# A block's closing waits, moved in front of the last stores

## The chip, the cores and the metric

The kernel runs on one core of a Trainium2 chip. Such a core has five engines that run side by side, each from an instruction stream of its own: TensorE (PE, matrix products), VectorE (DVE), ScalarE (ACT), GpSimd (POOL) and SyncE (SP). SP computes nothing here: it issues nearly all DMA transfers and waits on semaphores. A DMA transfer that is issued runs on its own; when it has landed, it raises the semaphore that its issuing instruction names.

The metric is device time in microseconds (us) of one execution, as the median of several runs.

## The reference

The kernel computes a transformer block in which attention and a gated feed-forward part read the same normalised input and are added to it. `x` is 2048 x 512 in bf16, with 32 heads of width 16 and a feed-forward width of 1792.

```python
xn = _layernorm(x)
q, k, v = split(xn @ wqkv)                      # 32 heads of 16
p = softmax((q @ k.T) / 4)                      # 2048 x 2048 per head
attn = (p @ v).reshape(S, D) @ wo
gate, up = xn @ W_gate, xn @ W_up               # 512 -> 1792
glu = (where(gate > 0, gate, 0) * up) @ W_down  # 1792 -> 512
out = x + attn + glu
```

## The kernel before, in words

The program is not written engine by engine. `Graph.op` collects operations with their engine, an assumed duration and their dependencies; `Graph.run` plays them through and so fixes one queue for each engine; `Graph.emit` turns the queues into instructions, with semaphores where an operation needs another engine's result. What a queue's order is, is therefore decided before the kernel runs, and each engine walks its queue in that order.

The queries are worked off in four blocks of 512 rows (`NB`), within a block four groups of eight heads (`NGG`), each in two halves, and in each of those 16 tiles of 128 keys (`NT`). For each tile PE makes scores (`score`), ACT or, for a part of the tiles, DVE and POOL make the exponentials, and PE multiplies those with the values (`pv_stream`). Between these, as filler, PE does the projections, the gated feed-forward products and the output rows of the block before.

The output is stored in 16 tiles of 128 rows. Twelve of them, those of the first three blocks, are stored from SP's queue in the course of the kernel (`out_rows`, the store at L1122). The last four belong to the last block and form the kernel's tail (`normalise_last`, L1190 and on): for each tile the last product is added to what was accumulated, on DVE for three tiles (L1246) and by an ACT copy for the fourth (L1242). The three DVE tiles are stored by SP (L1256), the fourth by ACT's own queue (L1253, because `OWN_STORE = (3,)`).

Each transfer on SP belongs to a *stream*, a name that stands for one semaphore. A transfer that has no named stream gets one of its own (the weights and the input tiles, 50 with the eight transposing transfers); those that recur share a few: `("q", v, h)` for the query pieces (8), `("wu", k)` and `("wg", k)` for the feed-forward weights (8), `("n1", n)`, `("n2", n)`, `("n3", n, j)` for the softmax sums (24), `("pk", j, n)` for the packed heads (8), `("xr", m)` for the residual rows (4), `("out", m)` for the twelve earlier stores (8), and `("out", m, k)`, with three parts, for the three stores of the tail. That makes 113 streams on SP, and the ACT store has a semaphore of its own, `d_st0`: 114 in all.

A kernel must not end before its transfers have landed. `emit` sees to that with the list `fin`: one wait for each of the 114 semaphores, at that semaphore's final value. `play("SP", ...)` gives these waits to SP after the last operation of its queue (L560 to L562):

```python
            if e == "SP":
                for s, v in fin:
                    eng.wait_ge(s, v)
```

The program's end, an exchange of semaphores among all engines, carries line L564 in the profile, since that is where the block of engine programs opens.

Of the kernel before, what the change touches and what calls it, by code (L numbers as in the profile page):

```python
# [133 lines left out]
class Graph:  # L134
# [296 lines left out]
    def emit(self, nc, es):  # L431
# [18 lines left out]
        def line(o):  # L450
            return o.stream if o.eng == "SP" else "PEhi" if o.eng == "PE" and o.half else o.eng
        for e in self.ENGS:
            n = {}
# [10 lines left out]
        streams = {}  # L464
        while left:
            moved = False
            for e in self.ENGS:
                q = self.queue[e]
                while pos[e] < len(q):
                    o = q[pos[e]]  # L470
# [4 lines left out]
                    if e == "PE" and o.wsrc and o.load is not None:  # L475
                        o.wwaits = []
                        for d in sorted(o.wsrc, key=lambda d: -d.seq):
                            c = line(d)
                            v = d.val if d.eng == "SP" else d.cseq
# [7 lines left out]
                    for d in sorted(o.deps, key=lambda d: -d.seq):  # L487
                        c = line(d)
                        v = d.val if d.eng == "SP" else d.cseq
# [22 lines left out]
        dsem = {s: es.enter_context(nc.semaphore("d_%d" % i)) for i, s in enumerate(streams)}  # L512
        for e in self.ENGS:
            v = {}
            for o in self.queue[e]:
# [5 lines left out]
                elif o.signal:  # L521
                    v[line(o)] = v.get(line(o), 0) + 1
                    o.sem = (sems[line(o)], v[line(o)])
        fin = [(dsem[s], 16 * n) for s, n in streams.items()]
        stores = [o for o in self.queue["ACT"] if o.name == "st"]
        for i, o in enumerate(stores):
            fin.append((es.enter_context(nc.semaphore("d_st%d" % i)), 16))
# [2 lines left out]
        def play(e, eng):  # L530
            def wait(ds):
                best = {}
                for d in ds:
                    s, v = d.sem
                    if id(s) not in best or best[id(s)][1] < v:
                        best[id(s)] = (s, v)
                for s, v in best.values():
                    eng.wait_ge(s, v)
            loaded = set()
            for i, o in enumerate(self.queue[e]):  # L540
                if e == "PE" and o.load and o not in loaded:
                    wait(o.wwaits)
                    o.load(eng)
                if e == "PE" and o.load is not None and o.waits:

                    for q in self.queue[e][i + 1:i + 1 + self.AHEAD_LOADS]:
                        if q.load is None or q.wwaits or q in loaded:
                            break
                        if q.half != o.half:
                            if q.load:  # L550
                                q.load(eng)
                                loaded.add(q)
                            break
                wait(o.waits)
                ins = o.fn(eng)
                if e == "SP" or o.name == "st":
                    ins.then_inc(o.sem[0], 16)
                elif o.signal or o.pair is not None:
                    ins.then_inc(o.sem[0], 1)
# [4 lines that stand above are left out]
        with nc.Block() as block:  # L564
            @block.sync
            def _(e):
                play("SP", e)

            @block.gpsimd
            def _(e):  # L570
                play("POOL", e)

            @block.vector
            def _(e):
                play("DVE", e)

            @block.scalar
            def _(e):
                play("ACT", e)

            @block.tensor
            def _(e):
                play("PE", e)
# [934 lines left out]
```

## Time and profile before

| | us |
|---|---|
| median of 3 runs without a profile | 693.67 |
| the runs' lowest and highest | 692.96, 693.94 |
| the profiled execution | 697.19 |
| span in it, from the first to the last instruction | 695.2 |
| PE busy | 680.9 (98% of the span) |
| ACT busy | 671.4 (97%) |
| DVE busy | 601.6 (87%) |
| POOL busy | 505.0 (73%) |

The clock granted to TensorE was 0.999 of full speed. The profiled execution's own time stands above its span by 2.0 us, and above the median of the runs by 3.5 us.

How to read it: a row of the timeline gives an instruction's start from the span's beginning and its length. Rows that begin with SPq or ACTq are instructions of that engine's sequencer: waits, branches and DMA issues, which are not counted as busy time. A wait appears in the profile as `EVENT_SEMAPHORE`. For a DMA issue the row has the time that issuing took; how long the transfer then needed until its semaphore was complete stands apart, as "DMA to landing", counted from the issue. A line such as L562 is the line of the kernel's source that made the instruction.

### The profile page before, as it was taken

To read this page: it belongs to the slowest core of one execution; us is meant where nothing else is said; L and a number is where in the kernel's file an instruction comes from. 1 tells how busy PE (TensorE), PEld (TensorE's weight loads), DVE (VectorE), ACT (ScalarE), POOL (GpSimd) and SP (SyncE) were. 2 spreads that over 40 slices of the span, in tenths; PEclk is the share of its full clock that TensorE was granted. 3 is DMA by queue.
4 is the path that set the end of the run, shared out by engine and by line. 5 is a ranking of instruction groups with operands and counts; after the bars stand their busy time and mean duration, and the time that the engine had idled before them with its cause. 6 is when DMAs were issued, how large, how long until landed. Compare 5 with 4: busy or idle time off the path is not lost.

```text
span 695.2 us, 46400 instructions
## 1 busy us (share of the span) xinstructions
PE 680.9 (98%) x22230; PEld 388.8 (56%) x20952; DVE 601.6 (87%) x1009; ACT 671.4 (97%) x733; POOL 505.0 (73%) x513
## 2 busy tenths in 40 slices
PE   8999999999999999999999999999999999999997
PEld 3546566566554566556654644556554455565754
DVE  8958899999999686899999778899998787898795
ACT  6999999999999999999999999999999999999993
POOL 3323678777789876788868877888878966787790
PEclk9999999999999999999999999999999999999999
DMA  7230111233201122110101111111100121121001
GB/s 213 57 57 21 38 45 32 50 103 92 65 15 31 43 58 48 27 47 21 39 12 28 46 50 54 31 40 34 36 16 19 39 73 46 50 50 33 21 16 41
DMA packets 55820, 31.87 MB, mean 46 GB/s; under 512 B 21196, under 2 KB 53644, under 8 KB 55628
## 3 DMA queue, kind: packets, MB, share of 16 engines
q1 hardware_dynamic: 55484, 28.79, 16.1%
q8 instruction: 169, 2.77, 1.7%
q14 instruction: 23, 0.19, 0.1%
q10 hardware_dynamic: 144, 0.13, 0.1%
HBM read 22.28 MB, written 2.35 MB: 35 GB/s over the span
## 4 chain that ended last, share of the span: by engine, by line
PE 73%; ACT 21%; DVE 4%; issue 1%; DMA 0%; DVEq 0%; POOL 0%
PE ps L129 72%; ACT ring L1465 21%; DVE qd L1418 2%; DVE stats L778 1%; DVE xn_sb L791 0%; DMA x_sb<-in_A_x_dram 0%; DVE mv L779 0%; DVE xnT L832 0%; DVE qd L1438 0%; PE ps L1202 0%; DVE qT L1014 0%; DVE xn_sb L1246 0%; DVE vare L771 0%; DVE up_sb L1078 0%; DVEq L564 0%
## 5 line engine op out<-in xcount | busy, mean ns | idle before, releaser
L1465 ACT ACTIVATE ring<-ps 128x1024 bf16<-128x1024 f32 x720 | 665.0, 1110 | 7.1 <-PE ps L129 6.1
L1434 POOL TENSOR_TENSOR qd<-qd,ints 128x512 int32<-128x512 int32 x450 | 454.3, 1041 | 145.4 <-DVE qd L1418 67.9
L129 PE MATMUL ps<-qT,kT 64*32 64x512 bf16 x8192 | 466.3, 375 | 1.7 <-issue 0.4
L1418 DVE TENSOR_SCALAR qd<-ps 128x512 int16<-128x512 f32 x608 | 396.0, 684 | 64.7 <-PE ps L129 59.7
L129 PE MATMUL ps<-qd,v_aug 64*32 64x512 bf16 x3648 | 296.2, 375 | 1.2 <-issue 0.8
L129 PE MATMUL ps<-ring,v_aug 64*32 64x512 bf16 x2880 | 252.6, 375 | 0.6 <-issue 0.3
L1398 PEld LDWEIGHTS <-kT 64*32 64x32 bf16 x7952 | 170.8, 92 | 122.9 <-issue 38.3
L1370 PEld LDWEIGHTS <-v_aug 64*32 64x32 bf16 x5488 | 135.1, 92 | 73.2 <-issue 12.9
L129 PE MATMUL ps<-xnT,wus 64*32 64x512 bf16 x1792 | 137.1, 375 | 0.0
L129 PE MATMUL ps<-xnT,wgs 64*32 64x512 bf16 x1792 | 135.8, 375 | 0.5 <-DVE up_sb L1078 0.2
L1438 DVE TENSOR_SCALAR qd<-qd 128x2048 int16<-128x2048 int16 x79 | 61.6, 792 | 1.7 <-PE ps L129 1.5
L862 PEld LDWEIGHTS <-wus 64*32 64x32 bf16 x1792 | 44.1, 92 | 23.2 <-issue 2.9
L862 PEld LDWEIGHTS <-wgs 64*32 64x32 bf16 x1792 | 44.0, 92 | 22.5 <-issue 2.9
L862 PEld LDWEIGHTS <-hT 64*32 64x32 bf16 x1792 | 43.4, 92 | 23.5 <-issue 4.0
L129 PE MATMUL ps<-Wd,hT 64*32 64x512 bf16 x768 | 55.7, 375 | 0.7 <-DVE qd L1418 0.6
L129 PE MATMUL ps<-Wk,hT 64*32 64x512 bf16 x512 | 41.9, 376 | 0.4 <-issue 0.4
L1078 DVE COPY up_sb<-ps 128x512 f32<-128x512 f32 x56 | 38.2, 682 | 3.6 <-PE ps L129 3.5
L1082 DVE SCALAR_TENSOR_TENSOR hT<-ps,up_sb 128x512 bf16<-128x512 f32 x56 | 38.2, 682 | 2.2 <-PE ps L129 1.9
L129 PE MATMUL ps<-Wv,hT 64*32 64x512 bf16 x512 | 40.1, 376 | 0.0
L129 PE MATMUL ps<-Wo_p,x_sb 64*32 64x512 bf16 x480 | 38.9, 375 | 0.0
L129 PE MATMUL ps<-xnT,Wq 64*32 64x512 bf16 x480 | 36.7, 375 | 0.0
L129 PE MATMUL ps<-xnT,Wk 64*32 64x512 bf16 x480 | 34.0, 375 | 0.1
(73 smaller groups left out, 262.8 us busy)
## 6 DMA issues: line engine op xcount, KB each, us to landing
wus<-in_B_W_up_dram SPq DMA_DIRECT2D x38, 128.0 KB, 2.7
wgs<-in_B_W_gate_dram SPq DMA_DIRECT2D x38, 128.0 KB, 2.6
rb<-rec_scr SPq DMA_DIRECT2D x124, 32.0 KB, 2.8
xr_sb<-in_A_x_dram SPq DMA_DIRECT2D x16, 128.0 KB, 2.3
qT<-qf SPq DMA_DIRECT2D x120, 16.0 KB, 2.6
out_dram<-xn_sb SPq DMA_DIRECT2D x15, 128.0 KB, 1.8
x_sb<-in_A_x_dram SPq DMA_DIRECT2D x8, 128.0 KB, 2.7
x_sb<-oT SPq DMA_DIRECT2D x60, 16.0 KB, 2.7
```

Of the source, the lines that this page charges most:

```text
L129: return e.add_instruction(mybir.InstMatmult(name=e.bass.get_next_instruction_name(), engine=mybir.EngineType.PE, ins=[e.lower_ap(x), e.lo ...
L778: G.op("DVE", 580, lambda e, m=m: e.bn_stats(stats[:, m, :], xs(m)), reads=[t_xm[m]], writes=[t_st], prio=pr, order=last_xn if m == 4 else ())
L862: e.ldweights(w()[rows, 32 * j:32 * j + 32], tile_position=(rows.start, 32 * j))
L1078: G.op("DVE", 603, lambda e: e.tensor_copy(up_sb[:, tup.slot, :], bank_of(tu)), reads=[tu], writes=[tup], prio=-590)
L1082: G.op("DVE", 603, lambda e: e.scalar_tensor_tensor(out=hT[:, th.slot, :], in0=bank_of(tg), scalar=0.0, in1=up_sb[:, tup.slot, :], op0=ALU ...
L1370: e.ldweights(vs(j), tile_position=(64 * half, 32 * j))
L1398: e.ldweights(ks(m), tile_position=(64 * half, 32 * m))
L1418: G.op("DVE", 601, lambda e, j=j, tx=tx: e.tensor_scalar(qd[:, tq.slot, 512 * j:512 * j + 512], ps[:, BANK[tx.slot], :], IBIAS[3], 0.0, op ...
L1434: G.op("POOL", POOL_NS / POOL_PIECES + 60, lambda e, x=x, n=n, c=slice(i * m, i * m + m): e.tensor_tensor(x().bitcast(I32)[:, c], raw().bi ...
L1438: G.op("DVE", 600, lambda e, n=n, x=x: e.tensor_scalar(x(), raw(), float(SHIFTS[n + 1]), None, op0=ALU.add), reads=[ti, tq], writes=[t], p ...
L1465: exp_ops[u] = G.op("ACT", 904, lambda e, tr=tr, k0=k0: e.activation(ring[:, tr.slot, :, :], ps[:, 4 * k0:4 * k0 + 2, :], ACTF.Exp, scale= ...
```

## The change

The list of closing waits is cut in two. `end` is the place in SP's queue of the first store of the tail, found by its stream's three parts. `late` holds the streams of everything from there on: the three SP stores of the tail. The final waits for all other streams, `done`, 110 of them, are given to SP ahead of that first tail store. Behind the last store stay four waits: those of the three SP stores, and that of the ACT store. The final values that are waited for are the same as before, and so is everything on the other engines.

```diff
-        fin = [(dsem[s], 16 * n) for s, n in streams.items()]
+
+        sp = self.queue["SP"]
+        end = next(i for i, o in enumerate(sp) if o.stream[0] == "out" and len(o.stream) == 3)
+        late = {o.stream for o in sp[end:]}
+        done = [(dsem[s], 16 * n) for s, n in streams.items() if s not in late]
+        fin = [(dsem[s], 16 * n) for s, n in streams.items() if s in late]
         stores = [o for o in self.queue["ACT"] if o.name == "st"]
         for i, o in enumerate(stores):
             fin.append((es.enter_context(nc.semaphore("d_st%d" % i)), 16))
@@
             for i, o in enumerate(self.queue[e]):
+                if e == "SP" and i == end:
+                    for s, v in done:
+                        eng.wait_ge(s, v)
                 if e == "PE" and o.load and o not in loaded:
```

## The prediction

> **What bounds the kernel now.** I read four views: the page for the whole, the chain that ended last for its final stretch, the timeline of the tail, and the rows of single source lines on SP. The page and the end of the chain first; the chain's columns are start, length, what.
>
> ```profile
> span 695.2 us, 46400 instructions
> PE 680.9 (98%) x22230; PEld 388.8 (56%) x20952; DVE 601.6 (87%) x1009; ACT 671.4 (97%) x733; POOL 505.0 (73%) x513
> ...
> PE 73%; ACT 21%; DVE 4%; issue 1%; DMA 0%; DVEq 0%; POOL 0%
> ...
> 689.61 0.68 DVE xn_sb L1246
> 690.29 0.60 DVEq L564
> ```
>
> PE bounds the body of the kernel, and the change does not touch the body. What the reader should see is that the chain stops at 690.29 + 0.60 = 690.89, while the span goes on to 695.2. The chain is followed through engine work, and in the last 4.3 us there is none. So the tail must be read by itself. Its timeline, with columns start, length, engine, line, operation:
>
> ```profile
> 689.01 1.88 DVE L1246 TENSOR_TENSOR xn_sb<-ps,xnT 128x512 bf16<-128x512 f32 x3
> 689.72 1.53 SPq L1256 DMA_DIRECT2D out_dram<-xn_sb  x3
> 690.24 0.60 ACT L1242 ACTIVATE xn_sb<-ps 128x512 bf16<-128x512 f32 x1 [5.07 <-PE ps L129]
> 690.87 0.40 ACTq L1253 DMA_DIRECT2D out_dram<-xn_sb  x1
> ```
>
> DVE's last add ends at 690.89 and the fourth tile's copy at 690.84; the ACT store is issued at 690.87, and SP is done issuing at 689.72 + 1.53 = 691.25. Now what SP does after that, and when the stores land. These are the rows of lines L562 (closing waits), L564 (the program's end), L1256 and L1253 (the SP stores and the ACT store); durations in ns as least, median, most:
>
> ```profile
> L562 SPq EVENT_SEMAPHORE  x57: 17/28/28, 691.3 to 694.7; - x57
> ...
> L564 SPq COMPARE_BRANCH  x1: 41/41/41, 694.8 to 694.8; - x1
> L564 SPq DRAIN  x1: 13/13/13, 695.0 to 695.0; - x1
> ...
> L1256 SPq DMA_DIRECT2D out_dram<-xn_sb x3: 332/357/357, 689.7 to 690.9; - x3
> DMA to landing us min/median/max: 1.7/1.7/2.0
> ...
> L1253 ACTq DMA_DIRECT2D out_dram<-xn_sb x1: 398/398/398, 690.9 to 690.9; - x1
> DMA to landing us min/median/max: 2.2/2.2/2.2
> ```
>
> The third SP store is issued at 691.25 - 0.33 = 690.92 and lands by 690.92 + 2.0 = 692.9. The ACT store lands at 690.87 + 2.2 = 693.1, the last landing of the kernel. But SP is still in its waits until 694.7. The 114 waits of the list appear as 57 recorded instructions, two waits to each. Are they held up by a landing, or is it their number? The same line in slices of half a microsecond, and then the DMA traffic in slices of the tail (columns: length of the slice, granted clock, DMA share, GB/s):
>
> ```profile
> L562 SPq EVENT_SEMAPHORE  x9: 27/28/28, 691.7 to 692.2; - x9
> ...
> L562 SPq EVENT_SEMAPHORE  x8: 27/28/28, 692.2 to 692.7; - x8
> ...
> L562 SPq EVENT_SEMAPHORE  x9: 27/28/28, 693.2 to 693.7; - x9
> ...
> L562 SPq EVENT_SEMAPHORE  x9: 27/28/28, 694.2 to 694.7; - x9
> ...
> 692.20:692.70 0.50, 1.00 0.71 230
> 692.70:693.20 0.50, 1.00 0.00 0
> ```
>
> Eight or nine in each slice, while the stores run and long after all traffic has ceased at 692.7. None is held up. The walk has a steady pace of (694.7 - 691.3) / 56 = 61 ns, and 57 of them make 3.5 us. So the last stretch is set by the number of waits that SP goes through behind its last store, 1.6 us beyond the last landing (694.7 against 693.1).
>
> **The change, part by part.** *What leaves the end.* 110 of 114 waits, some 55 records, go. SP is free at 691.25 and then has four waits, two records. They wait for landings at 692.9 and 693.1, so the last one starts at about 693.1 and not at 694.7. From the last wait to the end of the span it was 695.2 - 694.7 = 0.5 us of branch, drain and exchange; that stays. New span: 693.1 + 0.5 = 693.6, which is 1.6 us less. What is late next is the ACT store's landing; waits cost nothing there as long as they take less than the 1.85 us from 691.25 to 693.1, and two take 0.12 us.
>
> *What is added in front.* The 55 records now stand in SP's queue ahead of the first tail store, and behind them are three stores only. SP's queue around that place, the reader of the last transfer that SP issued before, and how long those transfers took:
>
> ```profile
> 675.32 0.33 SPq L1309 DMA_DIRECT2D rec_scr<-rrec  x1
> 677.75 2.94 SPq L1316 DMA_DIRECT2D rb<-rec_scr  x4
> ...
> 682.28 1.28 POOL L1325 TENSOR_TENSOR x_sb<-o_sb,rb 128x512 bf16<-128x512 f32 x1 [4.46 <-DMA rb<-rec_scr]
> ...
> L1316 SPq DMA_DIRECT2D rb<-rec_scr x4: 331/421/1641, 677.8 to 679.0; - x4
> DMA to landing us min/median/max: 1.7/3.1/3.3
> ```
>
> SP issues nothing between 677.75 + 2.94 = 680.69 and 689.72. The four `rb` transfers are the last ones before the tail; the last is issued at 680.69 - 1.64 = 679.05 and lands by 679.05 + 3.3 = 682.35. POOL, which waited for them, starts at 682.28, which agrees. Every other stream's last transfer was issued earlier still. So at worst SP stands until 682.35 at a wait, and then walks all 55: 55 x 0.061 = 3.4 us, to 685.7. The first tail store can be issued at 689.72, when DVE's first add is done. Cost on the path: nothing, with 4.0 us to spare. Should that cover be gone, each microsecond that SP arrives late would move the stores.
>
> *The store's own wait.* The first store also waits for DVE. Standing behind 110 others, that wait may become a record of its own, which I bound by nothing and one pace of 61 ns. The first store would then go at 689.78. The third, which is the late one of the three, goes when DVE ends at 690.89, and two issues of 0.36 us in front of it leave room: 689.78 + 0.72 = 690.50. Nothing again. No DMA is added or moved to another queue; PE, ACT, DVE and POOL have the same streams.
>
> *The sum, and what is not known.* In the profiled execution: 697.19 - 1.6 = 695.6 us. The median of the runs, 693.67, is 3.5 us lower than this execution, so something in it takes less time unrecorded, and the pace of SP's waits can be part of that. Its bounds: 61 ns is the pace as recorded. From below, an instruction's own recorded 28 ns, if all of the 33 ns between two were recording; then the walk is 57 x 0.028 = 1.6 us and ends before the last landing, and nothing is gained. I take 61 ns, since these rows are the very instructions that move. On the other side, landings: the SP stores' least was 1.7 us; if the ACT store too took 1.7 and not 2.2, the last landing would be 690.92 + 1.7 = 692.6, and the gain 2.1 us. Applied to the median: 693.67 - 1.6 = 692.1 us.
>
> [...]
>
> **The rivals.** *First: the waits are faster when nothing is recorded.* The gain is the walk less 1.85 us, so it vanishes at a pace of 1.85 / 57 = 32 ns. At the middle of the bounds, (28 + 61) / 2 = 45 ns, the walk is 2.6 us, the gain 0.7 us, and the time 693.0; at 32 ns and below it is 693.67. For it: the 3.5 us between the profiled execution and the median. Against it: those 3.5 us could lie anywhere among 46400 recorded instructions, and a pace as low as 32 ns would need half of it to lie in these 57. [...]
>
> *Second, slower: a transfer in `done` lands late and holds the first tail store back.* Its place is the 55 records before L1256. If SP comes through them at time W, three issues follow at some 0.40 us each, so the third starts at W + 0.8 and lands at W + 2.8. The stores move once W is over 689.72, and the kernel is slower than before when W + 2.8 is over 694.7, thus W over 691.9, instead of 685.7. Beyond that it costs 1 us for each. If the `rb` landing were 7 us later than recorded, 693.67 + 0.8 = 694.5 us. Against it: the most that `rb` took was 3.3 us, and POOL's start at 682.28 would have moved as well.
>
> *That it does nothing at all* (the waits end up in the same place) is the far end of the first rival: 693.67.
>
> **How the numbers follow.** The forecast, the full recorded pace, gets 0.60: it is read off the instructions concerned, and needs only that recording adds little. Its own range is 691.6 (landings at 1.7) to 692.7 (a pace of 51 ns: walk 2.9, gain 1.0). The first rival gets 0.34, the second 0.06. The runs of before scatter from 692.96 to 693.94, so the low end goes a little below 691.6, to 691.4, and the high end takes in the first rival with no gain, 693.7. About 0.2% (1.4 us) is what a measurement of this kernel can tell from no change, and 1.6 us is only just over it. Of the forecast's 0.60 I count 0.51 as over that bound, and of the first rival 0.04: faster 0.55. Slower is the second rival, 0.06. The rest, 0.39, is within the bound.
>
> **What would show it.** In the changed kernel's profile: two records in place of 57 at the old place behind the last store; some 55 on SP after 680.7, at 61 ns, with at most a stop until 682.35, and over by 685.7; the first SP store still at about 689.7; the end of the span 0.5 us after the ACT store's landing; the span at 693.6. The profiled spans would differ by 1.6 us in either case; it is the unrecorded times that tell forecast and first rival apart. The prediction is wrong if the runs without a profile gain clearly less than the span does, if a store starts later than before, or if the last landing moves.

## The result, and the profile after

The changed kernel takes 691.35 us (median of 22 runs, 689.2 to 693.79), the kernel before, run beside it, 692.86 us (median of 22, 691.51 to 693.94). The ratio is 0.9978, with a 95% interval from 0.9969 to 0.9987: 1.5 us less, between 0.9 and 2.1. The gain forecast was 1.6 us. The forecast time of 692.1 us was too high all the same, and the measured one lies 0.05 us below the stated range of 691.4 to 693.7.

The page of the changed kernel's profiled execution (691.42 us, near its median), first lines:

```profile
span 689.4 us, 46402 instructions
## 1 busy us (share of the span) xinstructions
PE 679.4 (99%) x22232; PEld 390.2 (57%) x20952; DVE 601.9 (87%) x1009; ACT 669.5 (97%) x733; POOL 505.0 (73%) x513
```

The span is 5.8 us shorter than the 695.2 of before, far more than the runs differ. To see which part of this is the change, the tail's timeline (start, length, engine, line, operation), and the end of the chain that ended last:

```profile
684.86 1.88 DVE L1254 TENSOR_TENSOR xn_sb<-ps,xnT 128x512 bf16<-128x512 f32 x3
...
685.64 1.46 SPq L1264 DMA_DIRECT2D out_dram<-xn_sb  x3
686.09 0.60 ACT L1250 ACTIVATE xn_sb<-ps 128x512 bf16<-128x512 f32 x1 [5.06 <-PE ps L129]
686.72 0.40 ACTq L1261 DMA_DIRECT2D out_dram<-xn_sb  x1
...
686.14 0.60 DVEq L572
```

DVE's tail begins at 684.86, and at 689.01 before: 4.15 us of the difference had arisen ahead of the tail, where nothing was changed. From the end of the last add the count is another: here 684.86 + 1.88 = 686.74, and 2.7 us from there to the end of the span; before, 690.89 and 4.3 us. The tail is 1.6 us shorter. As before, the chain stops where the last add ends (its last piece is DVE's closing drain, which ends at the same 686.74), and none of these 2.7 us is in it.

Now the rows of single lines, as for the kernel before. L548 are the waits in front, L543 has the wait that belongs to the first store, L570 the waits left behind the last store, L572 the program's end; then the SP stores and the ACT store:

```profile
L548 SPq EVENT_SEMAPHORE  x54: 27/28/28, 675.6 to 680.6; - x54
...
L543 SPq EVENT_SEMAPHORE  x2: 17/22/28, 167.0 to 685.6; - x2
...
L570 SPq EVENT_SEMAPHORE  x2: 17/22/28, 688.8 to 689.0; - x2
...
L572 SPq COMPARE_BRANCH  x1: 41/41/41, 689.0 to 689.0; - x1
...
L1264 SPq DMA_DIRECT2D out_dram<-xn_sb x3: 332/356/356, 685.6 to 686.8; - x3
DMA to landing us min/median/max: 1.8/1.8/2.0
...
L1261 ACTq DMA_DIRECT2D out_dram<-xn_sb x1: 398/398/398, 686.7 to 686.7; - x1
DMA to landing us min/median/max: 2.2/2.2/2.2
```

Behind the last store two records are left where there were 57. By the trace's semaphores the first record of such a list holds one wait, every other record two, and the branch the last one: 1 + 2 + 1 are the four waits here, and 1 + 56 x 2 + 1 the 114 before. The first starts at 688.8, when the third SP store has landed (686.77 + 2.0), the second at 689.0, when the ACT store has (686.72 + 2.2 = 688.9). What ends the kernel now is a landing, and 0.4 us of branch and exchange. The 54 records in front begin at 675.6, behind the last `rb` issue; SP stands ahead of the second of them until 677.2, when an `rb` transfer has landed, and ahead of each of the next two for 0.1 us more, at the landings of two more; they are over at 680.6, 5.0 us before the first store, and the one at 685.6 holds that store's own wait for DVE, which the issue itself held before. Its issue has become 0.07 us later against the add that it waits for; the third store, which matters, goes when its add ends, as before.

### The profile page after: what moved, and what is told of

It is laid out like the page before. It is cut to its first block, busy times and chain, and to the rows that moved or that the text cites. A ratio compares the mean times of both kernels' runs of the same rounds, so it can differ in the third digit from the quotient of the medians.

```text
span 689.4 us, 46402 instructions
## 1 busy us (share of the span) xinstructions
PE 679.4 (99%) x22232; PEld 390.2 (57%) x20952; DVE 601.9 (87%) x1009; ACT 669.5 (97%) x733; POOL 505.0 (73%) x513
## 4 chain that ended last, share of the span: by engine, by line
PE 72%; ACT 22%; DVE 4%; issue 1%; DMA 0%; DVEq 0%; POOL 0%
PE ps L129 72%; ACT ring L1473 22%; DVE qd L1426 2%; DVE stats L786 1%; DVE xn_sb L799 0%; DMA x_sb<-in_A_x_dram 0%; DVE mv L787 0%; DVE xnT L840 0%; DVE qd L1446 0%; PE ps L1210 0%; DVE qT L1022 0%; DVE vare L779 0%; DVE xn_sb L1254 0%; DVE up_sb L1086 0%; DVEq L572 0%
## 5 line engine op out<-in xcount | busy, mean ns | idle before, releaser
L1378 PEld LDWEIGHTS <-v_aug 64*32 64x32 bf16 x5488 | 133.5, 92 | 68.5 <-issue 11.1
```

The costliest lines, as they stand in the source:

```text
L1378: e.ldweights(vs(j), tile_position=(64 * half, 32 * j))
```

## The experiments

The measure for the tail is the time from SP's last store issue to the end of the span: 695.2 - (689.72 + 1.53) = 3.9 us in the kernel before, 689.4 - (685.64 + 1.46) = 2.3 us in the changed one. Theory A is the prediction's: behind the last store, the end is set by the later of two things, the walk through the waits at 61 ns for each record of two, and the last landing.

**The waits gone through four times.**

```diff
             if e == "SP":
                 for s, v in fin:
                     eng.wait_ge(s, v)
+                for _ in range(3):
+                    for s, v in fin:
+                        eng.wait_ge(s, v)
```

> The kernel before, with its 114 closing waits gone through four times behind the last store: 342 waits more, 171 records. Theory A (what SP does behind its last store sets the end, at the recorded 61 ns for two waits): 171 x 0.061 = 10.4 us more, a ratio of 1.015 to the kernel before, about 703.3 us; from SP's last store issue to the end of the span 3.9 + 10.4 = 14.3 us. Theory B (the first rival: outside of the profile a record takes 32 ns or less): at most 171 x 0.032 = 5.5 us more in the timed runs, a ratio of at most 1.008.

Measured: 704.07 us, against 691.74 for the kernel before beside it; ratio 1.0176, interval 1.0158 to 1.0194, thus 12.2 us more, between 10.9 and 13.4. The tail's rows, the waits as a whole, the waits in three stretches of time, the ACT store with its landing, and a line of the DMA view from 690 us to the end (queue, kind, packets, MB, share):

```profile
span 704.6 us, 46573 instructions
...
686.33 1.53 SPq L1259 DMA_DIRECT2D out_dram<-xn_sb  x3
...
L565 SPq EVENT_SEMAPHORE  x228: 17/28/1742, 687.9 to 704.1; - x114
...
L565 SPq EVENT_SEMAPHORE  x2: 17/880/1742, 687.9 to 688.0; - x2
...
L565 SPq EVENT_SEMAPHORE  x6: 28/28/28, 693.2 to 693.5; - x6
...
L565 SPq EVENT_SEMAPHORE  x5: 28/28/28, 693.9 to 694.2; - x5
...
L1256 ACTq DMA_DIRECT2D out_dram<-xn_sb x1: 397/397/397, 687.5 to 687.5; - x1
...
DMA to landing us min/median/max: 2.2/2.2/2.2
...
q14 instruction: 2, 0.02, 0.4%
```

The tail is 704.6 - 687.86 = 16.7 us, 12.8 more than before and not 10.4. The rest is not pace. One record, the second, took 1742 ns: in the program as built, the waits are laid out from the middle of the list outward, and in a list repeated four times the middle holds the ACT store's wait, so SP first stood 1.7 us until that store had landed (687.5 + 2.2 = 689.7) and then began to walk. In the kernel before, that wait comes last, and landing and walk overlap. Another 0.6 us are two short stops such as the one between 693.5 and 693.9, where no record starts. 10.4 + 1.7 + 0.6 = 12.7. The timed runs show a cost of that size too. At 32 ns for a record (theory B), even with these stops, it would be 5.5 + 2.3 = 7.8 us, a ratio of 1.011, which the interval excludes. For the times measured here the first rival falls. What is not shown is the pace in an execution with nothing recorded: each of these four runs has a span of its own on record, some 2 us below its time, and the profiled execution is one of the four.

**Where the walk stops counting.** The waits divided otherwise, in two kernels: in one, 54 of the 110 are left behind the last store; in the other, with 84 for 54 in both places of this diff, 84 are. Each was executed once, and only its trace is read:

```diff
-                    for s, v in done:
+                    for s, v in done[54:]:
                         eng.wait_ge(s, v)
@@
-                for s, v in fin:
+                for s, v in done[:54] + fin:
                     eng.wait_ge(s, v)
```

> The changed kernel, but only 56 of the 110 waits stand in front of the first tail store; 54 stay behind the last store beside the four: 29 records there. Theory A (the end is the later of walk and last landing): the walk is 29 x 0.061 = 1.8 us, as long as the last landing takes anyway, so from SP's last store issue to the end of the span it stays at the 2.3 us of the changed kernel, 0.1 us more at most. Rival (each record behind the last store costs its pace): 27 records more than the changed kernel has, 1.6 us more, 3.9 us.

> The changed kernel, but only 26 of the 110 waits in front of the first tail store, and 88 behind the last store: 44 records. Theory A: the walk now ends after the last landing; 44 x 0.061 = 2.7 us and the 0.46 us around it (3.93 less 57 x 0.061 in the kernel before) give 3.1 us from SP's last store issue to the end of the span. Rival (any walk that begins while a store is on its way is hidden by it): 2.3 us.

With 54 left behind:

```profile
span 688.4 us, 46402 instructions
...
684.65 1.46 SPq L1264 DMA_DIRECT2D out_dram<-xn_sb  x3
...
L570 SPq EVENT_SEMAPHORE  x29: 17/28/28, 686.2 to 688.0; - x29
```

With 84 left behind:

```profile
span 688.2 us, 46400 instructions
...
683.62 1.46 SPq L1264 DMA_DIRECT2D out_dram<-xn_sb  x3
...
L570 SPq EVENT_SEMAPHORE  x44: 17/28/28, 685.1 to 687.7; - x44
```

29 records: 688.4 - 686.11 = 2.3 us, as in the changed kernel with its two. 44 records: 688.2 - 685.08 = 3.1 us. Both as theory A has it, and neither rival. The line from 44 records (3.1) to 57 (3.9) falls at 0.8 / 13 = 62 ns for each; it meets the flat 2.3 us at 44 - 0.8 / 0.061 = 31 records. By this estimate, that is the point up to which waits behind the last store are free in this kernel.

**Waits left out and not moved.** Only the stores to the output need a closing wait for the output's sake.

```diff
-        fin = [(dsem[s], 16 * n) for s, n in streams.items()]
+        fin = [(dsem[s], 16 * n) for s, n in streams.items() if s[0] == "out"]
```

> The kernel before, with closing waits only for the twelve semaphores of the stores to the output, all behind the last store; the other 102 waits are in no place at all (their transfers are all read by work that the output depends on, the computation is whole). Theory A: six records, 0.4 us, lie within the last landing, so the time is that of the changed kernel: a ratio of 0.998 to the kernel before, 2.3 us from SP's last store issue to the end of the span. Rival (it is the waits in front of the stores that do something, and not that they are gone from the end): the changed kernel's gain is missing, ratio 1.000.

```profile
span 687.7 us, 46351 instructions
...
683.84 1.53 SPq L1256 DMA_DIRECT2D out_dram<-xn_sb  x3
...
L562 SPq EVENT_SEMAPHORE  x6: 17/28/28, 685.4 to 687.2; - x6
```

Ratio 0.9983, interval 0.9971 to 0.9994; tail 687.7 - 685.37 = 2.3 us. The same gain without a single wait in front. What the change does is that it takes waits away from the end; where they go is of no account as long as they are hidden.

**When they are not hidden.**

```diff
                 if e == "SP" and i == end:
-                    for s, v in done:
-                        eng.wait_ge(s, v)
+                    for _ in range(4):
+                        for s, v in done:
+                            eng.wait_ge(s, v)
```

> The changed kernel, with the 110 waits in front of the first tail store gone through four times: 220 records. This is the second rival's point put to the test. Theory A: from the landing of the last rb transfer (677.2 in the changed kernel's trace) the walk takes 220 x 0.061 = 13.4 us, to 690.6, where the first store went at 685.6; the third goes 0.8 us after the first, at 691.4 in place of 686.8, so the end comes about 4.5 us later than in the changed kernel: about 695.9 us, a ratio of 1.004 to the kernel before. Rival (SP's time in front of the stores is free whatever it does): 691.4 us, a ratio of 0.998.

```profile
span 691.9 us, 46567 instructions
...
684.27 1.88 DVE L1255 TENSOR_TENSOR xn_sb<-ps,xnT 128x512 bf16<-128x512 f32 x3
...
686.12 0.37 ACTq L1262 DMA_DIRECT2D out_dram<-xn_sb  x1
688.59 1.34 SPq L1265 DMA_DIRECT2D out_dram<-xn_sb  x3
...
L549 SPq EVENT_SEMAPHORE  x219: 27/28/28, 674.5 to 688.5; - x110
```

Ratio 1.0030, interval 1.0019 to 1.0040: 2.1 us slower than before, where I had expected about 3 (695.9 against 692.86). The mechanism is as expected: the three stores stand behind the walk, the first goes at 688.59, right behind the last record, while its add had ended at 684.27 + 0.68 = 684.95. The start of the walk was wrong: with the list laid out from its middle, the repeated list does not begin with the `rb` waits, so SP did not stand until 677 but walked from 674.5 on, and was through at 688.5 and not at 690.6. The walk took 14.0 us and not 13.4, because two short stops like those above add 0.6. From the last add to the end it is 691.9 - 686.15 = 5.7 us, 3.0 more than in the changed kernel. So the second rival is a real cost, which the changed kernel is clear of by 5.0 us.

**Both kernels once more.**

> The kernel before, unchanged, for a second profile and more runs. Theory A: from SP's last store issue to the end of the span 3.9 us again, since the tail is a fixed walk; the first store's issue, 689.7 us in the first profile, will differ by a microsecond or more, because the place at which the executions of one kernel differ is the body. Rival (the 5.8 us between the two profiled spans came from the change): first store again at 689.7 within 0.5 us.

> The changed kernel, unchanged, on the same chip. Theory A: 2.3 us from SP's last store issue to the end of the span, and a ratio of 0.998 to the kernel before (1.6 us less), whatever the level of the runs on this chip is.

The kernel before:

```profile
span 691.6 us, 46400 instructions
...
685.42 1.88 DVE L1246 TENSOR_TENSOR xn_sb<-ps,xnT 128x512 bf16<-128x512 f32 x3
...
686.13 1.53 SPq L1256 DMA_DIRECT2D out_dram<-xn_sb  x3
...
L562 SPq EVENT_SEMAPHORE  x57: 17/28/28, 687.7 to 691.1; - x57
```

The changed kernel:

```profile
span 690.5 us, 46400 instructions
...
685.96 1.88 DVE L1254 TENSOR_TENSOR xn_sb<-ps,xnT 128x512 bf16<-128x512 f32 x3
...
686.75 1.46 SPq L1264 DMA_DIRECT2D out_dram<-xn_sb  x3
...
L570 SPq EVENT_SEMAPHORE  x2: 17/22/28, 689.9 to 690.1; - x2
```

The tails are 691.6 - 687.66 = 3.9 us and 690.5 - 688.21 = 2.3 us, as in the first two profiles. The bodies are not: the first store of the unchanged kernel goes at 686.13 here and went at 689.72 there, 3.6 us apart with not an instruction different. In this pair the changed kernel's body is the longer one, by 0.6 us. So of the 5.8 us between the first two spans 1.6 are the change and 4.2 lie in the bodies, which differ by 3.6 in the unchanged kernel alone. The timed runs: changed kernel 0.9976 (0.9963 to 0.9989), which repeats the first result. The unchanged kernel, compared with itself, came out at 1.0011 (1.0001 to 1.0021): such an interval can miss the truth by 0.1%, half of this change's effect, and the trace of the tail is the sharper measure.

**A try at the rest.** Closing waits for the output stores alone, and one semaphore for all four tail stores:

```diff
-        dsem = {s: es.enter_context(nc.semaphore("d_%d" % i)) for i, s in enumerate(streams)}
+        dsem = {s: es.enter_context(nc.semaphore("d_%d" % i)) for i, s in enumerate(streams) if s[0] != "out" or len(s) < 3}
+        for s in streams:
+            if s not in dsem:
+                dsem[s] = sems.setdefault("late", None) or es.enter_context(nc.semaphore("d_late"))
+                sems["late"] = dsem[s]
...
-        done = [(dsem[s], 16 * n) for s, n in streams.items() if s not in late]
-        fin = [(dsem[s], 16 * n) for s, n in streams.items() if s in late]
+        done = [(dsem[s], 16 * n) for s, n in streams.items() if s[0] == "out" and s not in late]
...
+            o.sem = (sems["late"], 16)
+        fin = [(sems["late"], 16 * (len(late) + len(stores)))]
```

> A try at the rest: closing waits for the stores alone (the eight earlier ones in front of the first tail store), and all four stores of the tail raise one semaphore, so that one wait is left, on the end's branch. Theory A: the two records that stood between the last landing and the branch are gone, 0.1 us: 2.2 to 2.3 us from SP's last store issue to the end of the span, and a ratio of 0.998 to the kernel before, not to be told from the changed kernel in the timed runs. Rival (the end has more in it that hangs on the number of waits): clearly under 2.2 us.

```profile
span 689.4 us, 46347 instructions
...
685.63 1.46 SPq L1267 DMA_DIRECT2D out_dram<-xn_sb  x3
```

Tail 689.4 - 687.09 = 2.3 us; ratio 0.9983 (0.9973 to 0.9994). Not to be told from the changed kernel: the landing and the program's end are left, and no number of waits.

## Why the prediction was right or wrong

*The chain stops 4.3 us before the end, and the number of waits fills the gap.* Right. Four passes cost 12.2 us in the timed runs, and 44, 29, 6 and 2 records behind the last store gave 3.1, 2.3, 2.3 and 2.3 us.

*61 ns for a record.* Right, by the slope of 62 ns between 44 and 57 records and by the four passes, in the trace and in the measured times. The pace with nothing recorded stays open, as said above.

*Gain in the profile of 1.6 us, the ACT store's landing next.* Right: 4.3 us less 2.7 us from the last add to the end, in both pairs of profiles, and the last wait starts when that store has landed.

*No cost in front, 4.0 us to spare.* Right; 5.0 us in the changed kernel's profile, with SP standing at `rb` landings until 677.5, which the prediction allowed for. *The store's own wait may become a record.* It did, and cost nothing that the end saw.

*"Applied to the median: 693.67 - 1.6 = 692.1 us", and the low end "a little below 691.6, to 691.4".* This is the step that failed. The term that was off is the base, not the gain. 693.67 was a median of three runs; over 22 runs, those three among them, the kernel before has 692.86, and beside the later runs 691.74 and 691.11 (on two different chips by the record, so this further fall may be the chips'). I had read the scatter of three runs, 692.96 to 693.94, as the scatter of the kernel, and let the low end take 0.2 us of it. The base alone moved by 0.8 us, and 692.86 less the predicted 1.6 would have been 691.3, beside the measured 691.35. The other ground of the low end, an ACT store that lands in 1.7 us, did not come true either: it took 2.2 us in both profiles of the changed kernel. That the measured time lies only 0.05 us outside the range is luck: the low end reached so far down by a landing that did not come.

*The first rival's ground: the profiled execution was 3.5 us above the median, "so something in it takes less time unrecorded".* Not borne out as a reading. The unchanged kernel's second profile, recorded just as well, had a span 3.6 us shorter with the same tail, so the excess of the first lies in the body and not in the waits. Why that body was so long is open: 697.19 is above every other time of this kernel on record (693.94 at most), and in later sets the profiled execution, which is counted among the runs, was the slowest in some and not in others. As a ground for giving that rival 0.34 it was weak.

## What to carry to other kernels

Count what stands behind the last store: where a kernel ends with one wait for each semaphore it has used, that list is work on one engine, here 3.5 us for 57 records. In this kernel it cost time once it took longer than the last landing: with 29 records the tail took 2.3 us, with 44 it took 3.1 (by the estimate above, the limit is at 31). Put such waits where their engine idles (tail 2.3 us here), or leave out those that other work has already waited for (2.3 us as well); but see that no store is queued behind them when it becomes ready, which here cost 3.0 us with four passes in front. For a change this small, read the stretch that it touches in two profiles instead of the whole spans, and take the level of a forecast from more than three runs.

## What the runs showed of the hardware

SP went through satisfied waits at 61 ns for a record with two of them, of which 28 ns are the record's own duration. In the long runs of such records there were short stops in which none starts: with four passes, 693.5 to 693.9 and once more 8 us later, 0.6 us beyond the pace together. In the same stretch the DMA view has two transfers of the kind "instruction" on q14 and no other traffic; each is of 8 KB and starts 0.6 us after the end of a stop, and in the run with four passes in front the same is seen twice. That the stops have to do with these transfers is a guess from the times; what makes SP stand there was not shown.

The duration shown for a wait was once that of standing at it: 1742 ns for one that ended with a landing. In another case it was not: in the changed kernel SP stood 1.6 us at an `rb` landing in front, and this is a gap between two records of 28 ns each, at 675.6 and 677.2.

The ACT store landed 2.2 us after its issue where SP's three stores ran beside it (both profiles of both kernels, and the run with four passes), and in 1.7 us where they were issued 2.5 us behind it (the waits in front gone through four times). So this store landed quicker when it ran alone; the reason was not tried.

Two executions of the same kernel, with the granted clock at 0.999 in both, differed by 3.6 us in the body, while their tails agreed within 0.1 us. Where in the body this comes about was not settled.
